# wq loaded first, output sums in two column groups of 288, and the output stored as two plain halves

## The chip, the cores and the metric

The kernel runs on one core of one Trainium2 chip. The core has a matrix engine (PE), a vector engine (DVE), a scalar engine (ACT), GpSimd (POOL) and a sync engine (SP), each with its own instruction queue, and 16 DMA engines that move data between the off-chip memory and the on-chip memory SBUF. PE writes its sums to a second on-chip memory, PSUM. The metric is the device time of one launch in microseconds (us). The kernel before takes 134.05 us, the median of three runs (133.94 to 134.16).

## What is computed

A decode step for two sequences (B = 2, one token each, D = 576): a layer norm, then attention over a sliding block of a cached K and V, plus a dense block with a squared ReLU, plus the input itself.

```python
xn = _layernorm(x)                                   # (2, 1, 576)
# A: 32 query heads of 128, 16 K/V heads, the last W = 2048 of 8192 cached positions
q = (xn @ wq).reshape(B, Sq, Hq, Dh).transpose(0, 2, 1, 3)
k = jnp.repeat(k_cache[:, :, Sk - W:, :], rep, axis=1)
v = jnp.repeat(v_cache[:, :, Sk - W:, :], rep, axis=1)
p = softmax(einsum("bhqd,bhkd->bhqk", q, k) * Dh ** -0.5)
o = einsum("bhqk,bhkd->bhqd", p, v)
a = o.transpose(0, 2, 1, 3).reshape(B, Sq, Hq * Dh) @ wo
# B: F = 4608
h = xn @ w1 + b1
b = square(relu(h)) @ w2 + b2
return x + a + b
```

All inputs and the output are bf16. K and V of the block are 2 x 16.8 MB, wq and wo 4.7 MB each, w1 and w2 5.3 MB each: 53.6 MB are read for one output of 2 x 576.

## The kernel before

**Units.** K and V are worked on in eight units (NU = 8), each one batch entry and four K/V heads: 2048 positions x 4 heads x 128, a tile of 128 partitions x 16 KB (2 MB) for K and one for V. K and V tiles share a pool of six buffers (`kvpool`, line 85), so a load into a buffer waits until what it held has been used. `load_k` and `load_v` (lines 110 to 114) issue them on SP's queue.

**The queue of loads.** All large loads go on SP's queue in the order of the program. It begins (lines 130 to 136) with k0, wq, k1, v0, k2, v1, k3; v2 and k4 follow after units 0 and 1, and so on. A load carries a wait where its buffer is still in use or where the completion semaphore that it takes from a rotating set of eight is still held by an earlier transfer; what stands behind it on SP waits too. wq, w1 and wo use one buffer in turn (`wbig`, one buffer): w1 goes out when the query products are done, wo (line 435) when the products with w1 are done. Then come the two halves of w2: w2a (18 rows of 576), w2b (9 rows) and w2c in three pieces (6, 2 and 1 rows; W2P, line 76).

**Small transfers.** ACT issues x (line 125), four transfers for b1 (lines 417 and 418), one for b2, and the output (lines 455 and 457). Line 455 stores some of w2b to the output first, and line 457 then overwrites it with the result.

**Order on PE.** Every matmul and transpose is kept in program order. The program runs: the transposes of unit 0 (lines 409 and 410), the query block (`q_block`, lines 226 to 255: 36 products with wq, the rows copied, four transposes, eight copies that place the queries into qz), the scores of unit 0, its softmax, then the steps of units 1 to 6. In a step (`step`, line 387) the K tile is transposed in eight groups (line 264, copied out by ACT and DVE in turn at lines 270 and 272), the products with V of the unit two back are put in between (`pv`), and the scores and the softmax of the unit follow. `mlp_h` (line 356) does the products with w1, squares them and transposes them into hT_sb. After step 7, `pv_all` finishes the last two units, and each unit's result is written to ws (line 351).

**The output sums.** `out_acc` (lines 216 to 219) adds one row of wo or w2, a product of 576 columns, to the sums in PSUM. It splits the 576 columns into four quarters of 144 (OQ, line 81) and gives each to another group of 32 columns of the PE array, so that four products run beside each other; quarter i lands on partitions 32i and up. The two batch entries stand 16 rows apart (BS, MB; lines 78 and 79), so the left operands ws, hT_sb and sel_b have 17 columns, of which 15 are zero. The sums of b2 and x start the accumulation (line 422). Lines 445 to 451 do the 32 rows of wo, the 18 rows of w2a and the 18 rows of w2b and w2c. ACT then casts the 113 x 144 sums to bf16 (line 456), and one transfer of eight pieces of 288 bytes writes them out (line 457).

Of the kernel before, what the change touches and what calls it, by code (L numbers as in the profile page):

```python
# [8 lines left out]
F32 = mybir.dt.float32  # L9
BF16 = mybir.dt.bfloat16  # L10
ACT = mybir.ActivationFunctionType
ALU = mybir.AluOpType
AX = mybir.AxisListType
# [3 lines left out]
def kernel(  # L17
# [14 lines left out]
    nc = tc.nc  # L32
    P = 128
    B, Sq, D = A_x.shape
    _, Hkv, Sk, Dh = A_k_cache.shape
# [25 lines left out]
    NG4 = 4  # L61
# [10 lines left out]
    WR = Hq * Dh // P  # L72
    WC = Dh // WR
    FR = L1 // P
    assert HW == 32 * FR and QH * 2 == NC and NC * WC == 32
    W2P = [(9, 15), (15, 17), (17, 18)]
    R9 = 9
    BS = 16
    MB = BS * (B - 1) + 1
    RM = 32 * (NG4 - 1) + MB  # L80
    OQ = D // 4
    BIG = 1e30

    const = ctx.enter_context(tc.tile_pool(name="const", bufs=1))
# [4 lines left out]
    work = ctx.enter_context(tc.tile_pool(name="work", bufs=2))  # L89
    keep = ctx.enter_context(tc.tile_pool(name="keep", bufs=2))  # L90
    psum = ctx.enter_context(tc.tile_pool(name="psum", bufs=1, space=bass.MemoryType.PSUM))

    def matmul(*a, **k):
        tc.keep_in_program_order(nc.tensor.matmul(*a, **k))  # L94
# [5 lines left out]
    out2d = out.rearrange("b s d -> (b s) d")  # L100
# [9 lines left out]
    def load_k(u):  # L110
        issue_kv(k_tiles, A_k_cache, u, "k")
# [4 lines left out]
    def issue_flat(w, name):  # L116
        n = w.shape[0] * w.shape[1] // P
        tl = wbig.tile([P, NH * L1], BF16, tag="wbig", name=name)
        nc.sync.dma_start(out=tl[:, 0:n], in_=w.rearrange("r n -> (r n)").rearrange("(p l) -> p l", p=P))
        return tl  # L120
# [6 lines left out]
    nc.vector.memset(eps_t[:], 1e-5)  # L127
    warm = const.tile([B, 2], F32, name="warm")
    nc.scalar.activation(out=warm[:, 0:1], in_=eps_t[:], func=ACT.Sqrt)
    load_k(0)  # L130
    wq_sb = issue_flat(A_wq, "wq")
    load_k(1)
    load_v(0)
    load_k(2)
# [14 lines left out]
    ident = const.tile([P, P], BF16, name="ident")  # L149
    nc.vector.tensor_scalar(out=ident[:], in0=col_f, scalar1=row_f[:, 0:1], scalar2=None, op0=ALU.is_equal)  # L150
    ident_f = const.tile([P, P], F32, name="ident_f")
    nc.vector.tensor_scalar(out=ident_f[:], in0=col_f[:], scalar1=row_f[:, 0:1], scalar2=None, op0=ALU.is_equal)
    sel_b = const.tile([B + 1, MB], BF16, name="sel_b")
    nc.vector.memset(sel_b[:], 0.0)
    nc.vector.memset(sel_b[:, 0:MB:BS], 1.0)
    nc.vector.tensor_copy(out=sel_b[0:B, 0:MB:BS], in_=ident[0:B, 0:B])

    half_d = D // 2
    stats = const.tile([B, 2, 6], F32, name="stats")
# [50 lines left out]

    w2c_sb = w2pool.tile([P, (FR - R9) * D], BF16, name="w2c")

    out_ps = psum.tile([RM, OQ], F32, tag="out", name="out_ps")
    nc.vector.memset(out_ps[:], 0.0)

    def out_acc(lhsT, rhs, o, start=False, stop=False):
        for i in range(4):
            matmul(out_ps[32 * i:32 * i + MB, :], lhsT=lhsT, rhs=rhs[:, o * D + i * OQ:o * D + (i + 1) * OQ],
                   start=start, stop=stop, skip_group_check=True, tile_position=(0, 32 * i))

    qz = const.tile([P, NQ, B, 2, 3 * QZ], BF16, name="qz")
    nc.gpsimd.memset(qz[:], 0.0)
    q_ps = psum.tile([P, QW], F32, tag="o", name="q_ps")
    nc.vector.memset(q_ps[:], 0.0)

    def q_block():
        for t in range(NH):
            for g in range(NG4):
                o = t * LQ + g * QW
                matmul(q_ps[32 * g:32 * g + 2 * B, :], lhsT=xnT[:, t].rearrange("p x b -> p (x b)"),  # L230
                       rhs=wq_sb[:, o:o + QW], start=(t == 0), stop=(t == NH - 1), skip_group_check=True,
                       tile_position=(0, 32 * g))
        row_t = const.tile([RB, 4 * HW], BF16, tag="row", name="qrow")
        qrow = row_t[:, 0:2 * QW]
        nh = QH // 2
        for k in range(2):
            cp = nc.scalar.copy if k else nc.vector.tensor_copy
            cp(out=qrow[:, k * QW:(k + 1) * QW].rearrange("p (i a d) -> p i a d", a=2, d=Dh),  # L238
               in_=q_ps[0:RB, k * QW // 2:(k + 1) * QW // 2].rearrange("p (i d) -> p i d", d=Dh).unsqueeze(2)
               .to_broadcast([RB, nh, 2, Dh]))  # L240
        qrow_f = qrow.bitcast(F32)
        qT_ps = psum.tile([P, QH * P], F32, tag="sc", bufs=2, name="qT_ps")
        for i in range(QH):
            transpose(out=qT_ps[:, i * P:i * P + RB], in_=qrow_f[:, i * Dh:(i + 1) * Dh],
                      identity=ident_f[0:RB, 0:RB])
        qT_v = qT_ps[:].bitcast(BF16).rearrange("p (i g e x b c) -> p b x g c e i", g=NG4 // 2, e=2, x=32 // B, b=B, c=2)
        hd = Dh // 2
        for j2 in range(2):
            cp = nc.scalar.copy if j2 else nc.vector.tensor_copy
            pp = slice(hd * j2, hd * (j2 + 1))  # L250
            o = QZ + NC * j2
            for b in range(B):
                for half in range(2):
                    cp(out=qz[pp, half * NQ // 2:(half + 1) * NQ // 2, b, :, o:o + NC].rearrange(  # L254
                        "p g c (e i) -> p g c e i", e=2), in_=qT_v[pp, b, half])
# [50 lines left out]
        pT_tiles[u] = pT  # L306
        o1_tiles[u] = o1

    ws = const.tile([P, WR, MB], BF16, name="ws")
    nc.gpsimd.memset(ws[:], 0.0)  # L310
    hT_sb = const.tile([P, 2, FR, MB], BF16, name="hT_sb")
    nc.gpsimd.memset(hT_sb[:], 0.0)

    def pv(u, part, parts):
        n = NJJ // parts
# [10 lines left out]
    def pv_end(u):  # L326
        tq, b = divmod(u, B)
        o_ps = o_tiles.pop(u)
        o1 = o1_tiles.pop(u)
        for k in range(NS):  # L330
            kw = dict(out=o1[:, 0:Dh], in0=o_ps[:, k * Dh:(k + 1) * Dh])
            if k == 0:
                nc.vector.tensor_scalar(scalar1=in_s[:, 0:1], scalar2=None, op0=ALU.mult, **kw)
            else:
                nc.vector.scalar_tensor_tensor(scalar=in_s[:, k:k + 1], in1=o1[:, 0:Dh], op0=ALU.mult, op1=ALU.add,  # L335
                                               **kw)

        def fin():
            op = psum.tile([P, Dh + 1], F32, tag="op", name=f"op_ps_{u}")
            pp = slice(32 * tq, 32 * (tq + 1))  # L340
            matmul(op[pp, :], lhsT=of_h[:], rhs=o1[:], start=True, stop=True, skip_group_check=True,
                   tile_position=(0, 32 * tq))
            linv = work.tile([P, 1], F32, tag="linv", name=f"linv_{u}")
            nc.vector.reciprocal(out=linv[pp, :], in_=op[pp, Dh:Dh + 1])
            om_t = work.tile([P, Dh], F32, tag="om", name=f"om_{u}")
            om = om_t[pp, :].rearrange("p (q r) -> p q r", r=WR)
            nc.vector.scalar_tensor_tensor(out=om, in0=op[pp, 0:Dh].rearrange("p (q r) -> p q r", r=WR),
                                           scalar=linv[pp, 0:1], op0=ALU.mult, op1=ALU.mult,
                                           in1=own_c[pp, :].unsqueeze(2).to_broadcast([32, WC, WR]))
            with nc.allow_low_precision(reason="sums of one term and zeros"):  # L350
                nc.vector.tensor_reduce(out=ws[pp, :, BS * b], in_=om.rearrange("p q r -> p r q"), axis=AX.X,  # L351
                                        op=ALU.add)

        return fin

    def mlp_h(w1_sb):
# [19 lines left out]
        nr = FR // 2  # L376
        for a in range(2):
            hp = psum.tile([P, nr, RB + 4], BF16, tag="sc", bufs=2, name=f"hp_{a}")
            for r in range(nr):
                transpose(out=hp[:, r, 0:RB], in_=hrow[:, a * nr + r:4 * HW:FR], identity=ident[0:RB, 0:RB])  # L380
            for g in range(NG4):
                pp = slice(32 * g, 32 * (g + 1))
                cp = nc.scalar.copy if g % 2 else nc.vector.tensor_copy
                cp(out=hT_sb[pp, :, a * nr:(a + 1) * nr, 0:MB:BS].rearrange("p x r b -> p r x b"),
                   in_=hp[pp, :, 32 * g:32 * g + 2 * B].rearrange("p r (x b) -> p r x b", b=B))

    def step(u):
# [17 lines left out]
    def pv_all(u):  # L405
        pv(u, 0, 1)
        pv_end(u)()

    for g in range(NG):
        transposes(0, g)  # L410
    q_block()
    for t in range(NT):
        scores(0, t)
    softmax(0)
    load_v(2)
    b1_rows = B_b1.rearrange("(x n) -> x n", n=HW)
    for i0, i1 in ((0, 2), (2, 4), (4, 6), (6, 8)):
        nc.scalar.dma_start(out=b1_sb[i0:i1, :], in_=b1_rows[i0:i1, :])
    nc.scalar.dma_start(out=xb_sb[B:B + 1, :], in_=B_b2.rearrange("(o n) -> o n", o=1))
    step(1)  # L420
# [21 lines left out]
    step(NU - 1)  # L442
    pv_all(NU - 2)
    pv_all(NU - 1)
    for r in range(WR):
        out_acc(ws[:, r, :], wo_sb, r)
    for r in range(FR):
        out_acc(hT_sb[:, 0, r, :], w2a_sb, r)
    for r in range(FR):
        w, o = (w2b_sb, r) if r < R9 else (w2c_sb, r - R9)  # L450
        out_acc(hT_sb[:, 1, r, :], w, o, stop=(r == FR - 1))

    fin_sb = work.tile([RM, OQ], BF16, tag="fin", name="fin_sb")
    out_v = out2d.rearrange("b (q n) -> q b n", q=4)
    nc.scalar.dma_start(out=out_v, in_=w2b_sb[0:RM:BS, 0:OQ])
    nc.scalar.copy(out=fin_sb[:], in_=out_ps[:])  # L456
    nc.scalar.dma_start(out=out_v, in_=fin_sb[0:RM:BS, :])


# [28 lines left out]
```

## Time and profile before

| what | value |
|---|---|
| median of three runs | 134.05 us (133.94 to 134.16) |
| span of the profiled execution | 132.06 us (shown as 132.1) |
| mean granted clock of PE | 0.834 |
| busy: PE, DVE, ACT, POOL | 84.6, 63.2, 46.7, 4.9 us |
| read from off-chip memory | 53.62 MB, 406 GB/s over the span |
| share of the large loads' queue | 95.2% of 16 engines' span |
| instruction fetches (queue q8) | 7 packets, 0.11 MB |
| unit 0: transposes, scores done | 8.08 to 14.37 us, 27.20 us |
| wq lands, query products | 19.2 us, 19.23 to 23.27 us |
| products with wo start | 118.36 us |
| cast of the sums, store issued | 129.29, 129.60 us |

The profile is one execution of the program on the chip. Its span runs from the first to the last instruction; a run's device time is about 2 us longer than the span. Times are in us from the start of the span unless marked ns. PE is the matmul stream and PEld the weight loads that run beside it; SP's and ACT's own transfers are listed as SPq and ACTq. A timeline line gives start, length, engine, line, operation, output <- inputs, shapes and count, and in brackets how long the engine was idle before it and what ended that. A line by stretches gives the stretch in us, its length, the busy time of PE, PEld, DVE, ACT and POOL (with the number of instructions), the granted clock of PE as a share of full speed, the busy share of the DMA engines and GB/s. The busy time of PE is made of modelled ends, so overlapping products count once.

### The profile page before, as it was taken

What the parts mean: (1) busy time and instruction counts of PE and PEld (TensorE: products, weight loads), DVE (VectorE), ACT (ScalarE), POOL (GpSimd) and SP (SyncE); (2) the same over time, 40 slices, a digit from 0 to 9 for tenths busy, and PEclk for the clock granted to TensorE, in tenths of its full rate; (3) what the DMA queues carried; (4) which work ended last, traced back from release to release, by engine and by line L of the source; (5) the groups of instructions that cost most, each with busy time, mean ns of one, the idle gap of its engine ahead of it and who ended that gap; (6) DMA issues with size and microseconds to landing.
All of it is one profiled execution on the core that took longest, in us unless ns stands there. A gap on an engine that the chain in (4) does not pass through costs nothing.

```text
span 132.1 us, 2285 instructions
## 1 busy us (share of the span) xinstructions
PE 84.6 (64%) x949; PEld 52.6 (40%) x949; DVE 63.2 (48%) x176; ACT 46.7 (35%) x67; POOL 4.9 (4%) x15
## 2 busy tenths in 40 slices
PE   0089319599589687697599787104819972739471
PEld 0069202286345353363455443002417640229360
DVE  7764400344557677396547687410075667550000
ACT  5725400339566085283256094200106632000000
POOL 5000000010010100100100100100000001000000
PEclk9999955959999999999779999855695999555955
DMA  4999899999999999999999999999999999899960
GB/s 160 397 437 526 369 388 442 422 432 432 429 432 422 442 417 427 437 432 437 432 427 414 437 488 402 445 424 405 427 427 442 468 435 458 376 408 418 418 255 1
DMA packets 3511, 53.76 MB, mean 407 GB/s; under 512 B 419, under 2 KB 558, under 8 KB 814
## 3 DMA queue, kind: packets, MB, share of 16 engines
q1 hardware_dynamic: 3456, 53.61, 95.2%
q8 instruction: 7, 0.11, 0.3%
q10 hardware_dynamic: 46, 0.02, 0.1%
q14 instruction: 2, 0.02, 0.0%
HBM read 53.62 MB, written 0.00 MB: 406 GB/s over the span
## 4 chain that ended last, share of the span: by engine, by line
DMA 78%; PE 15%; ACT 2%; SPq 1%; DVE 1%; issue 1%; ACTq 0%; DVEq 0%
DMA w<-in_B_w_dram 25%; DMA w2c<-in_B_w_dram 24%; DMA k<-in_A_k_cache_dram 16%; DMA wq<-in_A_wq_dram 13%; PE kT_ps L97 5%; PE h_ps L94 3%; PE q_ps L94 3%; PE sc_ps L94 2%; PE out_ps L94 1%; PE o_ps L94 1%; ACT kT L270 1%; DVE qrow L238 1%; SPq L106 0%; ACT qrow L238 0%; DVE qz L254 0%
## 5 line engine op out<-in xcount | busy, mean ns | idle before, releaser
L97 PE MATMUL kT_ps<-ident_f,k 128*128 128x128 f32 x256 | 41.4, 312 | 5.7 <-DMA k<-in_A_k_cache_dram 3.9
L97 PEld LDWEIGHTS kT_ps<-ident_f,k 128*128 128x128 f32 x256 | 32.9, 161 | 18.8 <-issue 9.9
L270 ACT COPY kT<-kT_ps 128x1024 bf16<-128x1024 bf16 x32 | 31.9, 1012 | 17.8 <-PE kT_ps L97 17.8
L272 DVE COPY kT<-kT_ps 128x1024 bf16<-128x1024 bf16 x32 | 21.8, 682 | 6.4 <-PE kT_ps L97 6.1
L94 PE MATMUL sc_ps<-kT,qz 128*32 128x512 bf16 x128 | 9.9, 388 | 6.7 <-DVE kT L272 4.7
L302 ACT ACTIVATE p<-sc_ps,bias 128x512 bf16<-128x512 f32 x8 | 5.5, 688 | 21.4 <-DVE gown L298 18.2
L94 PE MATMUL o_ps<-v,pT 128*32 128x512 bf16 x128 | 11.2, 429 | 0.0
L94 PEld LDWEIGHTS <-xnT 128*4 128x4 bf16 x108 | 3.5, 121 | 16.8 <-issue 15.2
L94 PE MATMUL h_ps<-w,xnT 128*4 128x288 bf16 x72 | 4.3, 429 | 8.0 <-DMA w<-in_B_w_dram 8.0
L305 DVE STREAM_TRANSPOSE pT<-p 128x512 bf16<-128x512 bf16 x8 | 5.7, 710 | 6.2 <-ACT p L302 6.2
L335 DVE SCALAR_TENSOR_TENSOR o<-o_ps,in_s,o 128x128 f32<-128x128 f32 x24 | 8.3, 345 | 0.4
L291 DVE TENSOR_REDUCE m<-sc_ps 128x1 f32<-128x512 f32 x8 | 5.5, 692 | 4.8 <-PE sc_ps L94 4.8
L375 DVE TENSOR_TENSOR hrow<-t 100x1152 bf16<-100x1152 f32 x2 | 2.6, 1355 | 9.6 <-ACT t L373 9.6
L94 PE MATMUL q_ps<-wq,xnT 128*4 128x512 bf16 x36 | 4.0, 627 | 4.9 <-DMA wq<-in_A_wq_dram 4.9
L295 POOL PARTITION_ALL_REDUCE gmax<-m x8 | 2.9, 367 | 104.9 <-DVE m L293 104.9
L94 PE MATMUL op_ps<-o,of_h 128*32 128x129 f32 x16 | 3.7, 316 | 4.6 <-DVE o L335 4.6
L456 ACT CAST fin_sb<-out_ps 113x144 bf16<-113x144 f32 x1 | 0.3, 280 | 17.9 <-PE out_ps L94 17.9
L94 PEld LDWEIGHTS <-qz 128*32 128x32 bf16 x128 | 2.1, 94 | 10.4 <-DVE kT L272 7.2
L97 PE MATMUL pro_ps<-ident,xn_sb 2*128 2x2 bf16 x5 | 0.9, 182 | 6.8 <-DVE xn_sb L171 6.5
L94 PEld LDWEIGHTS <-hT_sb 128*17 128x17 bf16 x144 | 3.4, 108 | 3.6 <-issue 3.5
L94 PE MATMUL out_ps<-wo,ws 128*17 128x144 bf16 x128 | 4.0, 325 | 1.2 <-DVE ws L351 1.2
L238 DVE CAST qrow<-q_ps 100x512 bf16<-100x512 f32 x1 | 0.7, 692 | 8.2 <-PE q_ps L94 8.2
(71 smaller groups left out, 57.4 us busy)
## 6 DMA issues: line engine op xcount, KB each, us to landing
k<-in_A_k_cache_dram SPq DMA_DIRECT2D x8, 2048.0 KB, 21.0
v<-in_A_v_cache_dram SPq DMA_DIRECT2D x8, 2048.0 KB, 21.5
w<-in_B_w_dram SPq DMA_DIRECT2D x1, 5184.0 KB
wq<-in_A_wq_dram SPq DMA_DIRECT2D x1, 4608.0 KB, 17.8
wo<-in_A_wo_dram SPq DMA_DIRECT2D x1, 4608.0 KB
w2a<-in_B_w_dram SPq DMA_DIRECT2D x1, 2592.0 KB, 26.9
w2b<-in_B_w_dram SPq DMA_DIRECT2D x1, 1296.0 KB
w2c<-in_B_w_dram SPq DMA_DIRECT2D x1, 864.0 KB
```

The lines of the kernel that those rows point to most:

```text
L94: tc.keep_in_program_order(nc.tensor.matmul(*a, **k))
L97: tc.keep_in_program_order(nc.tensor.transpose(*a, **k))
L238: cp(out=qrow[:, k * QW:(k + 1) * QW].rearrange("p (i a d) -> p i a d", a=2, d=Dh), in_=q_ps[0:RB, k * QW // 2:(k + 1) * QW // 2].rearrang ...
L270: nc.scalar.copy(out=kT, in_=kT_ps[:])
L272: nc.vector.tensor_copy(out=kT, in_=kT_ps[:])
L291: nc.vector.tensor_reduce(out=m1[:], in_=sc_ps[:], axis=AX.X, op=ALU.max)
L295: nc.gpsimd.partition_all_reduce(gmax[:], m2[:], channels=P, reduce_op=ReduceOp.max)
L302: nc.scalar.activation(out=p_sb[:], in_=sc_ps[:], func=ACT.Exp, bias=bias[:, 0:1], scale=scale, accum_out=o1[:, Dh:Dh + 1])
L305: nc.vector.transpose(out=pT[:].rearrange("p j r -> p (j r)"), in_=p_sb[:])
L335: nc.vector.scalar_tensor_tensor(scalar=in_s[:, k:k + 1], in1=o1[:, 0:Dh], op0=ALU.mult, op1=ALU.add, **kw)
L375: nc.vector.tensor_tensor(out=h4[:, :, k * HB:(k + 1) * HB], in0=t4, in1=t4, op=ALU.mult)
L456: nc.scalar.copy(out=fin_sb[:], in_=out_ps[:])
```

## The change

- wq is loaded ahead of k0 on SP's queue. `q_block` is cut into `q_rows` (the products with wq) and `q_place` (the rest), and both run ahead of the transposes of unit 0.
- The four transfers for b1 become three (rows 0-3, 3-6, 6-8).
- The 16-row distance of the batch entries goes: ws, hT_sb and sel_b have 2 columns and no zeros, and the two memsets of ws and hT_sb on POOL go with them.
- `out_acc` splits a row into two halves of 288 columns on two groups of the array. The even rows of wo and w2a go to out_ps (partitions 0 and 32), the odd rows to a second tile, pre_ps (partitions 64 and 96), which is cleared by DVE.
- After the last row of w2a, ACT copies pre_ps to SBUF (pre_sb, cleared by POOL before), and two fp32 products with columns of the fp32 identity add it to out_ps.
- The rows of w2b and w2c all go to out_ps, on two groups. Between them stand three products of 512 columns into a tile that nothing reads (spin_ps).
- The sums are 34 x 288. The output goes as two transfers of two rows each, the first half on ACT's queue, the second on SP's; the earlier store of w2b into the output covers the first half only.

```diff
+    HD = D // 2
+    RO = 32 + B
+    RP = 96 + B
...
+    wq_sb = issue_flat(A_wq, "wq")
     load_k(0)
-    wq_sb = issue_flat(A_wq, "wq")
     load_k(1)
...
-    out_ps = psum.tile([RM, OQ], F32, tag="out", name="out_ps")
+    out_ps = psum.tile([RO, HD], F32, tag="out", name="out_ps")
     nc.vector.memset(out_ps[:], 0.0)
-    def out_acc(lhsT, rhs, o, start=False, stop=False):
-        for i in range(4):
-            matmul(out_ps[32 * i:32 * i + MB, :], lhsT=lhsT, rhs=rhs[:, o * D + i * OQ:o * D + (i + 1) * OQ],
-                   start=start, stop=stop, skip_group_check=True, tile_position=(0, 32 * i))
+    def out_acc(lhsT, rhs, o, start=False, stop=False, acc=out_ps, base=0):
+        for i in range(2):
+            p = base + 32 * i
+            matmul(acc[p:p + B, :], lhsT=lhsT, rhs=rhs[:, o * D + i * HD:o * D + (i + 1) * HD], start=start,
+                   stop=stop, skip_group_check=True, tile_position=(0, p))
...
-    ws = const.tile([P, WR, MB], BF16, name="ws")
-    nc.gpsimd.memset(ws[:], 0.0)
-    hT_sb = const.tile([P, 2, FR, MB], BF16, name="hT_sb")
-    nc.gpsimd.memset(hT_sb[:], 0.0)
+    ws = const.tile([P, WR, B], BF16, name="ws")
+    hT_sb = const.tile([P, 2, FR, B], BF16, name="hT_sb")
...
+    q_rows()
+    q_place()
     for g in range(NG):
         transposes(0, g)
-    q_block()
...
-    for i0, i1 in ((0, 2), (2, 4), (4, 6), (6, 8)):
+    for i0, i1 in ((0, 3), (3, 6), (6, 8)):
         nc.scalar.dma_start(out=b1_sb[i0:i1, :], in_=b1_rows[i0:i1, :])
...
+    pre_ps = psum.tile([RP, HD], F32, tag="sc", bufs=2, name="pre_ps")
+    nc.vector.memset(pre_ps[:], 0.0)
+    pre_sb = work.tile([P, HD], F32, tag="t1", name="pre_sb")
+    nc.gpsimd.memset(pre_sb[:], 0.0)
+    spin_ps = psum.tile([P, 512], F32, tag="sc", bufs=2, name="spin_ps")
+
+    def out_alt(lhsT, rhs, r, start=False, stop=False):
+        if r % 2:
+            out_acc(lhsT, rhs, r, start=start, stop=stop, acc=pre_ps, base=64)
+        else:
+            out_acc(lhsT, rhs, r)
+
     for r in range(WR):
-        out_acc(ws[:, r, :], wo_sb, r)
+        out_alt(ws[:, r, :], wo_sb, r, start=(r == 1))
     for r in range(FR):
-        out_acc(hT_sb[:, 0, r, :], w2a_sb, r)
+        out_alt(hT_sb[:, 0, r, :], w2a_sb, r, stop=(r == FR - 1))
+    nc.scalar.copy(out=pre_sb[64:RP, :], in_=pre_ps[64:RP, :])
+    for i in range(2):
+        p = 64 + 32 * i
+        matmul(out_ps[32 * i:32 * i + B, :], lhsT=ident_f[:, p:p + B], rhs=pre_sb[:], start=False, stop=False,
+               skip_group_check=True, tile_position=(0, 32 * i))
     for r in range(FR):
         w, o = (w2b_sb, r) if r < R9 else (w2c_sb, r - R9)
         out_acc(hT_sb[:, 1, r, :], w, o, stop=(r == FR - 1))
+        if r == R9 - 1:
+            for _ in range(3):
+                matmul(spin_ps[0:B, :], lhsT=ws[:, 0, :], rhs=wo_sb[:, 0:512], start=True, stop=True,
+                       skip_group_check=True)
-    fin_sb = work.tile([RM, OQ], BF16, tag="fin", name="fin_sb")
-    out_v = out2d.rearrange("b (q n) -> q b n", q=4)
-    nc.scalar.dma_start(out=out_v, in_=w2b_sb[0:RM:BS, 0:OQ])
+    fin_sb = work.tile([RO, HD], BF16, tag="fin", name="fin_sb")
+    nc.scalar.dma_start(out=out2d[:, 0:HD], in_=w2b_sb[0:B, 0:HD])
     nc.scalar.copy(out=fin_sb[:], in_=out_ps[:])
-    nc.scalar.dma_start(out=out_v, in_=fin_sb[0:RM:BS, :])
+    nc.scalar.dma_start(out=out2d[:, 0:HD], in_=fin_sb[0:B, :])
+    nc.sync.dma_start(out=out2d[:, HD:D], in_=fin_sb[32:RO, :])
```

More of the change, by code (lines that the diff above doesn't have):

```diff
@@ L77 @@
     R9 = 9
[L78 to L81, printed above, removed]
+    HD = D // 2
+    RO = 32 + B
+    RP = 96 + B
     BIG = 1e30
@@ L152 @@
     nc.vector.tensor_scalar(out=ident_f[:], in0=col_f[:], scalar1=row_f[:, 0:1], scalar2=None, op0=ALU.is_equal)
[L153 to L156, printed above, removed]
+    sel_b = const.tile([B + 1, B], BF16, name="sel_b")
+    nc.vector.memset(sel_b[:], 1.0)
+    nc.vector.tensor_copy(out=sel_b[0:B, :], in_=ident[0:B, 0:B])
     half_d = D // 2
@@ L224, with q_rows @@
     nc.vector.memset(q_ps[:], 0.0)
-    def q_block():
+    def q_rows():
         for t in range(NH):
@@ L232, in q_block, with q_place @@
                        tile_position=(0, 32 * g))
+    def q_place():
         row_t = const.tile([RB, 4 * HW], BF16, tag="row", name="qrow")
@@ L350, in fin @@
             with nc.allow_low_precision(reason="sums of one term and zeros"):
-                nc.vector.tensor_reduce(out=ws[pp, :, BS * b], in_=om.rearrange("p q r -> p r q"), axis=AX.X,
+                nc.vector.tensor_reduce(out=ws[pp, :, b], in_=om.rearrange("p q r -> p r q"), axis=AX.X,
                                         op=ALU.add)
@@ L383, in mlp_h @@
                 cp = nc.scalar.copy if g % 2 else nc.vector.tensor_copy
-                cp(out=hT_sb[pp, :, a * nr:(a + 1) * nr, 0:MB:BS].rearrange("p x r b -> p r x b"),
+                cp(out=hT_sb[pp, :, a * nr:(a + 1) * nr, :].rearrange("p x r b -> p r x b"),
                    in_=hp[pp, :, 32 * g:32 * g + 2 * B].rearrange("p r (x b) -> p r x b", b=B))
```

## The prediction

> **What bounds the kernel now.** I read the busy shares by slice first, then the chain that ended last.
>
> ```profile
> span 132.1 us, 2285 instructions
> PEclk9999955959999999999779999855695999555955
> DMA  4999899999999999999999999999999999899960
> GB/s 160 397 437 526 369 388 442 422 432 432 429 432 422 442 417 427 437 432 437 432 427 414 437 488 402 445 424 405 427 427 442 468 435 458 376 408 418 418 255 1
> DMA 78%; PE 15%; ACT 2%; SPq 1%; DVE 1%; issue 1%; ACTq 0%; DVEq 0%
> ```
>
> The transfer engines are full from the second slice to the last but two: 53.6 MB at about 430 GB/s. PE, DVE and ACT only have to keep up. What they do counts in two places: where a late consumer would leave the queue without work, and behind the last landing. The timeline and the tile view show that tail:
>
> ```profile
> 118.36 4.02 PE L94 MATMUL out_ps<-wo,ws 128*17 128x144 bf16 x128 [1.16 <-DVE ws L351]
> 122.73 1.05 PE L94 MATMUL out_ps<-w2a,hT_sb 128*17 128x144 bf16 x54 [0.35 <-DMA w2a<-in_B_w_dram]
> 125.29 0.48 PE L94 MATMUL out_ps<-w2a,hT_sb 128*17 128x144 bf16 x18 [1.51 <-issue]
> 125.82 1.26 PE L94 MATMUL out_ps<-w2b,hT_sb 128*17 128x144 bf16 x36
> 127.90 1.34 PE L94 MATMUL out_ps<-w2c,hT_sb 128*17 128x144 bf16 x36 [0.82 <-DMA w2c<-in_B_w_dram]
> L94 PE MATMUL out_ps<-w2c,hT_sb x36: 278/327/328, 127.9 to 129.0; 128*17 128x144 bf16 x36
> 125.80 0.65 ACTq L455 DMA_DIRECT2D out_dram<-w2b  x1
> 129.29 0.28 ACT L456 CAST fin_sb<-out_ps 113x144 bf16<-113x144 f32 x1 [17.85 <-PE out_ps L94]
> 129.60 0.54 ACTq L457 DMA_DIRECT2D out_dram<-fin_sb  x1
> ```
>
> PE has spare time here: it waits for w2a (0.35), for its own instructions (1.51, "issue") and for w2c (0.82). The w2b tile lands by 125.80, when the dummy store that reads it (L455) goes out. The 36 w2c products pace at 30 ns, so 1.08 us of work took 1.34: they waited inside for the second and third piece. The last four start at 129.0, so I put the last landing at 128.9 (an estimate from that start).
>
> Last, the same tail cut at the borders where the granted clock changes, and one earlier stretch:
>
> ```profile
> 115.48:118.90 3.42, 1.15 (x22) 0.76 (x26) 1.80 (x6) 0.00 (x0) 0.00 (x0) 0.50 0.94 406
> 118.90:122.31 3.41, 3.41 (x116) 3.27 (x109) 0.00 (x0) 0.00 (x0) 0.00 (x0) 0.50 0.98 420
> 122.31:125.72 3.41, 1.54 (x76) 1.15 (x72) 0.00 (x0) 0.00 (x0) 0.00 (x0) 1.00 0.98 409
> 125.72:129.14 3.42, 2.55 (x74) 2.08 (x71) 0.00 (x0) 0.00 (x0) 0.00 (x0) 0.50 0.55 215
> 129.14:132.10 2.96, 0.11 (x4) 0.00 (x0) 0.00 (x0) 0.28 (x1) 0.00 (x0) 0.50 0.00 1
> 50.63:54.04 3.41, 2.00 (x18) 0.89 (x16) 2.19 (x6) 1.01 (x1) 0.00 (x0) 1.00 0.99 423
> ```
>
> The first number after the stretch is its length, the next PE's busy time; 0.50 or 1.00 ahead of the last two is the granted clock. The clock steps every 3.41 us. At half clock a full stretch (3.41) lifts the next one to 1.00; 2.55, three quarters, did not. At full clock 1.54 (45%) dropped the next to 0.50, while after 2.00 (59%) it stayed at 1.00.
>
> **The change, part by part.** Times are in the profiled execution (span 132.06); the median of the runs is 134.05, so 1.99 us lie outside the span, taken as unchanged.
>
> *wq ahead of k0.* Same bytes on SP's queue. k0 and wq together landed at 19.2; at 430 GB/s k0's 2.1 MB are 4.9 us, so wq alone lands near 14.3. Query products (4.0, as now) end at 18.3; the placing took 25.98-23.27 = 2.7, to 21.0. Unit 0's transposes follow the last query transpose, near 20.1, and with their copies took 15.1-8.1 = 7.0: to 27.1. The scores (1.2, plus 0.4 for the mask product) end near 28.6 against 27.2: 1.4 us late. Queued behind on SP, v2 waits for the transposes of unit 0 (26.5 for 19.27) and k4 for those of unit 1 (about 35 for 33.63). At 33.63 19.4 MB have been issued and some 13.2 landed (31.5 us at 0.42 MB/us), so 6.2 MB or 14 us of transfers still cover a delay of 1.4. PE wins it back: it waits 0.32 for k at 44.77 and 1.22 at 54.63. Cost 0; if the cover were gone, +1.4. The b1 transfers, three for four, each saves some 0.3 us of issue on ACT at 4.4 us, where nothing waits: 0.
>
> *Smaller ws, hT_sb, sel_b.* Two POOL memsets (0.55 and 0.61) and one on DVE go, all in the first 2.5 us under the first load: 0. Two memsets are added: pre_ps on DVE (about 0.3, from 485 ns for 128x512) in unit 7 between accumulations, where DVE idles 0.78 before L344, and pre_sb on POOL, which idles: 0.
>
> *Two column groups.* The wo and w2a rows alternate between groups 0/1 and 2/3, four groups as before: half as many products of double width. From h_ps, 72 products of 288 columns in four groups in 4.30 us at half clock: 60 ns each, 240 alone. So wo is 64 x 60 = 3.84 (was 4.02), w2a 36 x 30 = 1.1 at full clock (the 72 ran at some 20 ns). The 1.51 "issue" is a wait for the instruction stream; 262 fewer loads and products in the tail may remove it (gain 0 to 1.51, all in PE's slack). The last half stays on two groups: 120 ns a product at half clock, 61 at full, against 2 x 30 and 2 x 16 before. w2b is 18 x 61 = 1.1 or 18 x 120 = 2.2; w2c the same.
>
> *Join.* ACT copies 34x288 (0.40: L373 does 100x288 in 404 to 411 ns), then two fp32 products. op_ps, 129 fp32 columns, took 0.41 at full clock, some 0.24 above a product's 0.17 tail (223 ns less 144 columns at 2.4 a ns, twice the 288 in 240 above); 288 columns make 0.53 + 0.17 = 0.7 if the two groups overlap, 1.2 if not. From w2a's end at 124.0: copy to 124.5, join to 125.2 or 125.7. That is before w2b lands at 125.80: 0. At half clock it ends at 126 to 127.
>
> *Three spin products.* 512 columns in one group: 427 ns at half clock (36 of q_ps in 4.0 on four groups), 213 at full. At full clock 125.8 + 1.1 + 0.64 = 127.5, under the landing at 127.9: 0. Then w2c: twelve products 0.73 to 128.6, when piece two is due, four to 128.9, and the last pair on the last landing as now. Its latency: 286 ns (288 columns, full) for 290 (144, half): 0.
>
> *Cast and store.* 34x288 for 113x144: from 280 ns (144) to 586 (512) is 0.83 ns a column, +0.12. The store's way from issue to landing: now 129.60 to between 131.2 and 131.4 (SP waits 2.3 us for it from the last w2c piece; POOL's closing starts at 131.4). A plain two-row transfer on ACT, xb_sb, was issued at 0.73 and SP went on behind it at 2.19: 1.46, 0.15 to 0.35 less. For the half on SP I have only issue times, 0.33 (L441) to 0.63 (the first k), against 0.54: -0.21 to +0.09, plus a hand-over of 0.05. Both halves must land. Ends -0.35 and +0.14; nearest is xb_sb, halved for the second half: -0.1.
>
> On the second queue the Trainium skill ("DMA: Bandwidth & Descriptors", Issuing engines are not separate DMA queues) speaks against a gain: two issuers save only issue time. By it the store's term would be 0 and the sum +0.12; no row here shows two stores at once.
>
> Sum: 0.12 - 0.1 = +0.02, so **134.1**. Its own range: -0.35+0.12 = -0.23 to 0.14+0.12+0.15 (last pair at half clock, 444 ns as in h_ps) = +0.41, and 0.11 of spread between runs: 133.7 to 134.6. Within 0.2% (0.27 us), about what a measurement can tell from none, I call no change.
>
> **The rivals.**
>
> *The clock is at half under w2b and w2c (slower).* That is the condition of the sum: PE's own time decides once the w2c products can't end by 129. If the clock falls only for w2c: 127.9 + 18 x 0.12 + 0.17 = 130.23 for 129.24, +1.0: 135.1. From w2b on: 125.8 + 2.16 + 1.28 of spin + 2.16 + 0.17 = 131.57, +2.35: 136.4. For it: in the profile the clock does stand at 0.50 from 125.72, harmless only because four groups hid it; the borders need not fall at the same place in each run, and a wo block of 3.9 us just fills one stretch of 3.41. If the lift needs over nine tenths, a border in mid-block misses it. Against: with the shorter idle times, w2a, join, w2b, spins and w2c make 1.25+0.7 busy in 122.3-125.7 (57%, near the 59% that held) and some 3.0 of 3.41 in the next. 0.35.
>
> On this the Trainium skill ("TensorE: Matmul & The Clock Gate", Part 1) drops the clock only after an idle window of about 3.4 us. By it the clock would hold from 122.3 on and the sum stand; the row at 45%, with no pause over 1.51, speaks otherwise, and the row decides.
>
> *The stream ends earlier (faster).* Instructions come over the same engines: seven packets, 0.3% of 16 engines' span (0.003 x 16 x 132.1 / 7 = 0.9 us of one engine each). With fewer of them the engine that ends last may end 0.9 earlier: 133.2; if they hit others, 0. 0.09.
>
> *The front's delay isn't won back.* +1.4 where the queue runs dry: 135.4; 14 us of issued work speak against it. 0.03.
>
> **How the numbers follow.** The sum's case has 0.53: 0.16 faster, 0.27 within, 0.10 slower (it runs from -0.34 to +0.52, the zone of no change in its middle). Clock 0.35, slower; early stream 0.09, faster; front 0.03, 0.02 of it slower and 0.01 within. Faster 0.25, same 0.28, slower 0.47. The range takes the first case, its faster edge and the clock's prices: 133.6 to 136.4.
>
> **What would show it.** w2c products start at 127.9 and the cast at 129.3, granted clock 1.00 from 125.8: the sum. A cast after 130 with 0.50: the clock. A w2c landing well before 127.9: the stream. DMA below 9 in slices 8 to 20: the front. Wrong altogether: a 288-column product on two groups slower than 61 ns, a join beyond 125.8, or an issue wait in the tail.

## The result and the profile after

| | kernel before | changed kernel |
|---|---|---|
| median (runs) | 134.05 us (5; 133.94 to 134.19) | 134.73 us (5; 134.61 to 134.88) |
| ratio to before, with 95% interval | | 1.0051 (1.0039 to 1.0063) |
| span of the profiled execution | 132.06 us | 132.74 us |
| last landing of the large loads, from the packet records | 128.56 us | 129.34 us |
| from there to the end of the span | 3.50 us | 3.40 us |
| mean granted clock of PE | 0.834 | 0.897 |

The changed kernel is slower by 0.68 us, 0.5%. The forecast of 134.1 was too low by 0.6 us; the range held the time. The two rows on the last landing (the end of the last packet of the large loads) already say where to look: behind it the change gains 0.10 us, and it comes 0.78 us later itself.

The page of the changed kernel, cut to the lines that were shown of before (span, shares by slice, the chain by engine):

```profile
span 132.7 us, 2025 instructions
PEclk9999999999999869999999999955595999655899
DMA  6898999999999999999999999998999999899970
GB/s 178 389 490 368 416 439 430 439 415 439 407 425 434 425 439 410 425 425 434 434 407 430 410 490 425 430 434 378 434 420 444 480 389 489 367 419 406 407 273 1
DMA 75%; PE 14%; ACT 5%; SPq 1%; issue 1%; DVE 1%; ACTq 0%; DVEq 0%
```

There are 260 instructions fewer and PE's clock is higher, but the transfer engines are as full as before and the chain that ended last still consists mostly of transfers (75%, before 78%). Nothing on this page names the loss. The tail (the products with w2 and what follows them), from the timeline of the changed kernel (start, length, engine, line, work, idle time before it):

```profile
123.48 0.40 PE L93 MATMUL out_ps<-w2a,hT_sb 128*2 128x288 bf16 x2 [0.48 <-DMA w2a<-in_B_w_dram]
...
125.09 0.39 ACT L461 COPY pre_sb<-pre_ps 34x288 f32<-34x288 f32 x1 [12.71 <-PE pre_ps L93]
125.54 0.65 PE L93 MATMUL out_ps<-pre_sb,ident_f 128*2 128x288 f32 x4 [0.56 <-ACT pre_sb L461]
126.61 0.26 ACTq L475 DMA_DIRECT2D out_dram<-w2b  x1
126.63 1.27 PE L93 MATMUL out_ps<-w2b,hT_sb 128*2 128x288 bf16 x18 [0.43 <-DMA w2b<-in_B_w_dram]
127.73 0.81 PE L93 MATMUL spin_ps<-wo,ws 128*2 128x512 bf16 x3
128.75 1.40 PE L93 MATMUL out_ps<-w2c,hT_sb 128*2 128x288 bf16 x18 [0.21 <-DMA w2c<-in_B_w_dram]
130.19 0.39 ACT L476 CAST fin_sb<-out_ps 34x288 bf16<-34x288 f32 x1 [4.70 <-PE out_ps L93]
130.61 0.33 SPq L478 DMA_DIRECT2D out_dram<-fin_sb  x1
130.61 0.25 ACTq L477 DMA_DIRECT2D out_dram<-fin_sb  x1
```

Each step waits for its load: w2a (0.48), w2b (0.43), w2c (0.21). The join ends at 126.19, before w2b's products; the spins end at 128.54, before w2c lands. The whole row is the one forecast, shifted: w2a 0.75, w2b 0.8 and w2c 0.85 later than before. The clock in this tail, by the stretches at whose borders it may change (columns as before: length, busy times of PE, PEld, DVE, ACT, POOL, granted clock, DMA share, GB/s):

```profile
120.58:123.99 3.41, 2.93 (x56) 1.55 (x48) 0.00 (x0) 0.00 (x0) 0.00 (x0) 0.50 0.96 404
123.99:127.40 3.41, 2.42 (x50) 1.26 (x44) 0.00 (x0) 0.39 (x1) 0.00 (x0) 1.00 0.99 400
127.40:130.81 3.41, 2.54 (x30) 1.24 (x25) 0.00 (x0) 0.39 (x1) 0.00 (x0) 1.00 0.30 113
```

The clock is 1.00 under the join, w2b, the spins and w2c, so the prediction's rival of a half clock did not happen.

Now the stream. These are products that wait for a load, in the kernel before:

```profile
54.63 1.06 PE L97 MATMUL kT_ps<-ident_f,k 128*128 128x128 f32 x8 [1.22 <-DMA k<-in_A_k_cache_dram]
74.12 1.06 PE L97 MATMUL kT_ps<-ident_f,k 128*128 128x128 f32 x8 [0.28 <-DMA k<-in_A_k_cache_dram]
91.09 4.27 PE L94 MATMUL h_ps<-w,xnT 128*4 128x288 bf16 x72 [7.96 <-DMA w<-in_B_w_dram]
```

and in the changed kernel:

```profile
54.94 1.06 PE L96 MATMUL kT_ps<-ident_f,k 128*128 128x128 f32 x8 [0.59 <-DMA k<-in_A_k_cache_dram]
74.56 1.06 PE L96 MATMUL kT_ps<-ident_f,k 128*128 128x128 f32 x8 [1.84 <-DMA k<-in_A_k_cache_dram]
91.67 4.49 PE L93 MATMUL h_ps<-w,xnT 128*4 128x288 bf16 x72 [8.78 <-DMA w<-in_B_w_dram]
```

Each starts at a landing, and the same landing is late by 0.31, then 0.44, then 0.58 us, then 0.75 for w2a. That is no pause at one place: from each of these points to the next the transfers are slower by 0.5 to 0.8%. The packet records (one for each piece that a transfer engine moves) say it directly. A K or V tile is 128 packets of 16 KB, eight for each of the 16 engines. From the 16th us on a packet took 611 ns in the kernel before; in the changed kernel 611 ns up to about 25 us and 615.7 ns after 40 us (means without the few packets that an instruction fetch held up). The packets of w1 rose from 1533.0 to 1537.8, those of wo from 1364.0 to 1368.6: 4.6 to 4.8 ns on each of these three sizes. The smaller packets of w2 rose by amounts from 0.5 ns (1152 bytes) to 8.2 ns (10368 bytes, 389.2 to 397.4). Some 165 packets per engine follow the 25th us; what they took longer, added up size by size, is 0.72 us of the 0.78.

Nor is it the engines that disturb the transfers. This stretch of the changed kernel has no work on any of them:

```profile
85.95:88.95 3.00, 0.00 (x0) 0.00 (x0) 0.00 (x0) 0.00 (x0) 0.00 (x0) 0.58 0.96 415
```

and yet w1's packets took 1539 ns in the mean between 86 and 89 us, against 1533 before.

What differs for a packet? Its bytes do not, and behind the first loads their order does not either. Its destination does. ws, hT_sb and sel_b lost 2080 bytes per partition, and everything allocated behind the constants moved down by that much: K and V buffers from byte 31232 of a partition (122 x 256) to 29152 (113 x 256 + 224), all with the same remainder since a buffer is 16 KB. The destinations of wq, w1, wo, w2b and w2c have that remainder too; w2a's went from 128 to 96. The unused tile `pad_0` (576 bytes, line 122 before, 121 after) lies ahead of the constants, so its size sets these addresses and nothing else.

### The profile page after: what moved, and what is told of

The parts are those of the page before. It is cut to its first block, busy times and chain, and to the rows that moved or that the text cites. A ratio compares the mean times of both kernels' runs of the same rounds, so it can differ in the third digit from the quotient of the medians.

```text
span 132.7 us, 2025 instructions
## 1 busy us (share of the span) xinstructions
PE 82.7 (62%) x818; PEld 45.7 (34%) x818; DVE 63.1 (48%) x176; ACT 46.7 (35%) x68; POOL 4.2 (3%) x14
## 4 chain that ended last, share of the span: by engine, by line
DMA 75%; PE 14%; ACT 5%; SPq 1%; issue 1%; DVE 1%; ACTq 0%; DVEq 0%
DMA w<-in_B_w_dram 25%; DMA w2c<-in_B_w_dram 23%; DMA k<-in_A_k_cache_dram 16%; DMA wq<-in_A_wq_dram 10%; PE kT_ps L96 4%; PE h_ps L93 3%; ACT kT L271 3%; PE q_ps L93 3%; PE sc_ps L93 2%; PE out_ps L93 1%; ACT L303 1%; PE o_ps L93 1%; DVE qrow L239 1%; ACT qrow L239 0%; SPq L105 0%
## 5 line engine op out<-in xcount | busy, mean ns | idle before, releaser
L96 PE MATMUL kT_ps<-ident_f,k 128*128 128x128 f32 x256 | 38.0, 290 | 7.6 <-DMA k<-in_A_k_cache_dram 5.6
L96 PEld LDWEIGHTS kT_ps<-ident_f,k 128*128 128x128 f32 x256 | 28.6, 146 | 22.1 <-issue 12.3
L93 PE MATMUL o_ps<-v,pT 128*32 128x512 bf16 x128 | 11.7, 451 | 0.0
L239 ACT CAST qrow<-q_ps 100x512 bf16<-100x512 f32 x1 | 0.6, 586 | 13.3 <-DVE qrow L239 13.3
L332 DVE TENSOR_SCALAR o<-o_ps,in_s 128x128 f32<-128x128 f32 x8 | 2.8, 346 | 5.1 <-PE o_ps L93 5.1
```

The lines of the kernel that those rows point to most:

```text
L96: tc.keep_in_program_order(nc.tensor.transpose(*a, **k))
```

## The experiments

Theory A: the packets became slower by their destination, that is, by the byte of a partition at which a load starts. Theory B: by the front, the new order at the start (wq first, K unit 2 held behind it), which might shift the 16 engines against each other. Medians are of 5 to 12 runs; the kernel before, run beside them, took 134.00, 134.01 and 134.02 us in the three sets.

**1. The changed kernel, tiles back on the old remainder.**

```diff
-    const.tile([P, 144], F32, name="pad_0")
+    const.tile([P, 536], F32, name="pad_0")
```

> The changed kernel with the unused pad of the constants' pool widened from 576 to 2144 bytes a partition, so that every K, V and weight tile starts 1568 bytes higher, on the same offset within 512 bytes as in the kernel before (0 for K and V; the changed kernel has 480). The instructions and their order are those of the change. Theory A (the stream's packets became slower since the smaller constants moved the destinations off 512-byte boundaries): the 16 KB packets take 611 ns all through, the last load lands about 0.8 us earlier, near 128.5 us of the span, and the time is about 133.95 us. Theory B (the new front, wq first and K unit 2 held back behind it, changed the phase of the 16 engines): packets of 617 ns after 26 us as in the change, 134.7 us.

133.75 us, ratio 0.9983 (0.9974 to 0.9992); last landing 128.55, packets of 611.0 ns. Waits for the same landings, and the end, in its timeline:

```profile
54.47 1.06 PE L96 MATMUL kT_ps<-ident_f,k 128*128 128x128 f32 x8 [0.24 <-DMA k<-in_A_k_cache_dram]
74.08 1.94 PE L96 MATMUL kT_ps<-ident_f,k 128*128 128x128 f32 x8 [1.91 <-DMA k<-in_A_k_cache_dram]
91.15 4.49 PE L93 MATMUL h_ps<-w,xnT 128*4 128x288 bf16 x72 [6.15 <-DMA w<-in_B_w_dram]
...
127.87 1.35 PE L93 MATMUL out_ps<-w2c,hT_sb 128*2 128x288 bf16 x18 [0.15 <-DMA w2c<-in_B_w_dram]
129.26 0.39 ACT L476 CAST fin_sb<-out_ps 34x288 bf16<-34x288 f32 x1 [4.07 <-PE out_ps L93]
```

The landings are those of the kernel before again (54.63, 74.12, 91.09, 127.90). An unused tile's size alone brings 0.98 us (0.91 by the two ratios to the kernel before, each run beside its own set) and puts the change on the other side of the kernel before.

**2. The kernel before, everything moved by 32 bytes.**

```diff
-    const.tile([P, 144], F32, name="pad_0")
+    const.tile([P, 136], F32, name="pad_0")
```

> The kernel before with the unused pad made 32 bytes smaller, so that K and V tiles start at offset 480 within 512 bytes, as the changed kernel has them; nothing else differs. Theory A (destination offsets): packets lengthen from 611 to about 617 ns, and the time rises to about 134.8 us. Theory B (order of the front): 134.05 us, within 0.15.

134.88 us, ratio 1.0068 (1.0055 to 1.0082); packets of 615.6 ns. The loss of the change without any of its work: theory A.

**3 and 4. The front taken out of the change, and put alone into the kernel before.** Number 3 has the order of the kernel before:

```diff
-    wq_sb = issue_flat(A_wq, "wq")
     load_k(0)
+    wq_sb = issue_flat(A_wq, "wq")
...
-    q_rows()
-    q_place()
     for g in range(NG):
         transposes(0, g)
+    q_rows()
+    q_place()
...
-    for i0, i1 in ((0, 3), (3, 6), (6, 8)):
+    for i0, i1 in ((0, 2), (2, 4), (4, 6), (6, 8)):
```

> The changed kernel with its front put back (K unit 0 ahead of wq, the q block behind the transposes of unit 0, the bias in four transfers), its smaller constants, its two column groups and its two-halves store kept. Theory A (destination offsets): still about 134.7 us, packets of 617 ns. Theory B (order of the front): 133.95 us, packets of 611 ns.

Number 4 is the reverse edit on the kernel before, whose `q_block` moves whole.

> The kernel before with only the front of the change (wq ahead of K unit 0, the q block ahead of the transposes of unit 0, the bias in three transfers); its constants, and so every tile's place, stay. Theory A (destination offsets): 134.05 us within 0.15, packets of 611 ns. Theory B (order of the front): about 134.8 us, packets of 617 ns after 26 us.

Number 3: 134.78 us, ratio 1.0059 (1.0046 to 1.0072), packets of 615.7 ns. Number 4: 133.95 us, ratio 0.9996 (0.9987 to 1.0005), packets of 611.0 ns. The slow packets go with the addresses and not with the front. Theory B falls.

**5. Only the destinations of the loads moved.** The kernel before with one unused 32-byte tile between the constants and the K/V buffers, and one behind the weights' buffers, so that the engines' own tiles move by 64 bytes and the constants not at all.

```diff
+    shift0 = ctx.enter_context(tc.tile_pool(name="shift0", bufs=1))
+    shift0.tile([P, 8], F32, name="shift_0")
     kvpool = ctx.enter_context(tc.tile_pool(name="kvpool", bufs=6))
...
+    shift1 = ctx.enter_context(tc.tile_pool(name="shift1", bufs=1))
+    shift1.tile([P, 8], F32, name="shift_1")
     ktpool = ctx.enter_context(tc.tile_pool(name="ktpool", bufs=2))
```

> The kernel before with two unused pads of 32 bytes, one ahead of the K and V buffers and one behind the weights' buffers: the destinations of the loads move by 32 bytes, the constants not at all, and the tiles that only the engines use by 64. Theory A (the destinations of the loads): about 134.88 us, as when everything moved by 32 bytes. Rival (what slows is an engine's read or write of its own tiles off a 64-byte boundary, or their clash with the loads): 134.0 us.

134.89 us, ratio 1.0064 (1.0052 to 1.0077), packets of 615.6 ns. Its waits for w1 and w2c:

```profile
91.64 4.07 PE L98 MATMUL h_ps<-w,xnT 128*4 128x288 bf16 x72 [7.79 <-DMA w<-in_B_w_dram]
...
128.72 1.39 PE L98 MATMUL out_ps<-w2c,hT_sb 128*17 128x144 bf16 x36 [0.87 <-DMA w2c<-in_B_w_dram]
```

These are the changed kernel's landings (91.67, 128.75) in the old kernel. The constants stayed, so it is the destinations of the loads. One rival isn't excluded by this run alone: the engines' own tiles moved by 64 bytes, and the engines read the loaded tiles at their new places. Against it stands the stretch from 85.95 us above, in which no engine worked and the packets were slow all the same.

**6 to 8. Which boundary.** The changed kernel with `pad_0` of 168, 184 and 216 floats.

> The changed kernel with its unused pad 96 bytes wider, so that K and V tiles start at offset 64 within 512 bytes (the changed kernel: 480; the widened one run before: 0). Theory A1 (a multiple of 64 bytes is enough for a destination): packets of 611 ns and about 133.75 us, as with offset 0. Theory A2 (only a multiple of 512, or of more than 64, will do): about 134.7 us.

> The changed kernel with its unused pad 160 bytes wider: K and V tiles start at offset 128 within 512 bytes. If a multiple of 128 bytes is enough (w2a's destination lies at offset 128 in the kernel before, and its packets of 20736 bytes took 771 ns there as in the widened kernel): 133.75 us, packets of 611 ns. If the step is at 512 bytes, or the cost falls off slowly with the offset's size: between 134.0 and 134.4 us.

> The changed kernel with its unused pad 288 bytes wider: K and V tiles start at offset 256 within 512 bytes. If a multiple of 128 or of 256 bytes is enough: 133.75 us. If only a multiple of 512 is: 134.0 to 134.4 us.

Together with the others, sorted by where in 256 bytes a K or V buffer starts:

| K/V start, remainder by 256 | kernel | 16 KB packets, ns | last landing, us | time, us | ratio to before (95%) |
|---|---|---|---|---|---|
| 0 | widened pad (1) | 611.0 | 128.55 | 133.75 | 0.9983 (0.9974 to 0.9992) |
| 0 (256 by 512) | pad 216 | 611.0 | 128.61 | 133.78 | 0.9975 (0.9966 to 0.9984) |
| 32 | loads moved (5) | 615.6 | 129.35 | 134.89 | 1.0064 (1.0052 to 1.0077) |
| 64 | pad 168 | 614.8 | 129.20 | 134.42 | 1.0031 (1.0019 to 1.0043) |
| 128 | pad 184 | 614.5 | 129.14 | 134.41 | 1.0022 (1.0009 to 1.0034) |
| 224 | the change | 615.7 | 129.34 | 134.73 | 1.0051 (1.0039 to 1.0063) |

The case "64 is enough" did not come true, and neither did "128 is enough". A multiple of 256 bytes costs nothing; 64 and 128 cost 3.5 to 3.8 ns a packet of 16 KB and about 0.65 us; 224, on the same instructions, 0.98 us. (Row 32 has the old instructions; number 2 is 224 on the old instructions, with 615.6 ns and 134.88 us.) It is the remainder and not the place: the fast starts 29440, 30720 and 31232 lie among slow ones, from 29152 (the change) to 31264 (number 5).

**9. Without the spins**, on the widened pad: the loop of three products is left out.

```diff
-        if r == R9 - 1:
-            for _ in range(3):
-                matmul(spin_ps[0:B, :], lhsT=ws[:, 0, :], rhs=wo_sb[:, 0:512], start=True, stop=True,
-                       skip_group_check=True)
```

> The changed kernel with the wide pad (133.75 us) without the three spin products between w2b and w2c. If the spins keep the clock: TensorE falls to half speed within 4 us of w2b's products, w2c's 18 products take about 2.0 in place of 1.4 us, and the time rises by 0.3 to 0.6 us, to 134.05 to 134.35. If the work of w2a, the join and w2b holds the clock by itself, or the last landing decides anyway: 133.75 within 0.15.

133.74 us (133.64 to 133.83 over 11 runs), ratio 0.9979 (0.9971 to 0.9988), against 133.75 with them. In its profile the clock was 1.00 from 121.65 to 131.89 without any spin. The spins change nothing here that these runs can tell.

**10. Without the second sum**, on the widened pad: all rows go straight to out_ps, no copy, no join.

```diff
-        if r % 2:
-            out_acc(lhsT, rhs, r, start=start, stop=stop, acc=pre_ps, base=64)
-        else:
-            out_acc(lhsT, rhs, r)
+        out_acc(lhsT, rhs, r)
```

> The changed kernel with the wide pad (133.75 us), with all rows of wo and w2a summed in the two column groups of the output, no second sum, no copy and no joining products. If the odd rows in groups of their own are needed: wo's 26 rows take 0.24 us each at half clock, some 6.2 us from about 120, w2a's 18 rows end about 128 and not 125.5, w2b's products follow late by 1 us or more, and the time is 134.0 to 135. If two groups suffice, since w2b and w2c are waited for anyway: 133.75 within 0.15.

134.38 us, ratio 1.0030 (1.0017 to 1.0043), 0.63 above its partner. The profiled execution is the longest of its eight (134.78 us; they run from 134.15), so its delays are larger than those of the median. From its timeline:

```profile
118.64 6.71 PE L93 MATMUL out_ps<-wo,ws 128*2 128x288 bf16 x64 [1.06 <-DVE ws L350]
125.19 2.37 PE L93 MATMUL out_ps<-w2a,hT_sb 128*2 128x288 bf16 x36
...
127.39 1.27 PE L93 MATMUL out_ps<-w2b,hT_sb 128*2 128x288 bf16 x18
...
130.46 0.39 ACT L464 CAST fin_sb<-out_ps 34x288 bf16<-34x288 f32 x1 [18.22 <-PE out_ps L93]
```

Behind the products with wo no line of PE has a wait in brackets: on two groups the rows of wo take 6.71 us (the prediction had 3.84 for four groups), those of w2a and w2b queue up behind them, and the cast is at 130.46 in place of 129.26. Alternating the rows over four groups is what lets two wide groups do in the rest of the tail.

**11. The tail without the front**, on the widened pad.

> The changed kernel with the wide pad and the front of the kernel before (K unit 0 ahead of wq, the q block behind the transposes, the bias in four transfers): what is left of the change is the two column groups, the join, the spins and the store, with every load on the offset of the kernel before. If the tail alone brings the 0.25 us of the widened kernel: 133.75 to 133.85 us. If the front brings it (the new front alone gave 133.95 against 134.00): 133.95 to 134.05.

133.94 us, ratio 0.9991 (0.9983 to 0.9999). On good addresses there are then four kernels: neither part 134.00 to 134.02, front alone 133.95, tail alone 133.94, both 133.75. Number 11 falls between the two cases of its expectation. The intervals are about 0.12 us wide to each side, so the front alone can't be told from nothing, the tail alone barely, and that both together bring 0.25 and not the 0.13 of their sum isn't clear of the noise either.

## Why the prediction missed, and why its range held

**The step that failed** is the line "Smaller ws, hT_sb, sel_b: ... 0", together with "Same bytes on SP's queue ... Cost 0". The first counted the memsets that go and not the 2080 bytes that go, which set the address of every load behind them; the second took equal bytes for equal time. In their place the runs show +0.98 us from the destination alone (the changed kernel against number 1), 0.7% of the time of a kernel that waits for its loads nearly throughout; the rest of the change brings -0.25 us (number 1 against the kernel before). The Trainium skill ("DMA: Bandwidth & Descriptors", How a descriptor splits into AXI transactions) describes such a boundary, for reads: a transaction has at most 256 bytes and must start on a multiple of 256, so that a descriptor which doesn't start there takes bytes that it doesn't use. The forecast drew on that page for the store and not for the loads. The runs agree on the boundary, for destinations in SBUF; on the size they don't follow the page's count of 32-byte beats, by which remainder 32 would be the cheapest and 224 the dearest, while 32 and 224 cost 4.6 and 4.7 ns on a packet of 16 KB, and 64 and 128 3.5 to 3.8.

**That the range held is luck.** The sum's own range ended at 134.6. The stated one reached to 136.4, and slower had the largest chance, for a half clock under w2b and w2c, which none of the eight profiles with the new tail and the join shows. The time lies in the range, and on its likeliest side, for a cause that stands in none of its cases.

**The sum behind the last landing was right in kind.** Forecast +0.02 (-0.23 to +0.41). From the last landing to the end, the four kernels profiled with the old tail took 3.50 to 3.63 us, mean 3.56, the eight with the new tail and the join 3.24 to 3.49, mean 3.35: -0.21, at the lower end. By terms, in the changed kernel: the cast +0.11 (0.28 to 0.39; forecast +0.12). The store, from issue to the end of the span, went from 132.06 - 129.60 = 2.46 to 132.74 - 130.61 = 2.13, so -0.33, near this term's lower bound of -0.35; I had taken -0.1. Whether this comes from two pieces in place of eight or from the second queue wasn't separated. Two readings of the kernel before were off, without weight for the result. The last landing, put at 128.9 by the start of the last four products, was at 128.56 by the packets: those products start at 128.95, 0.39 behind their last packet. And 131.57 us for the half clock from w2b on is 2.33 above 129.24, not 2.35.

**The join was hidden**, as forecast: 0.39 + 0.65 us, done 0.44 before w2b. The 1.51 us of "issue" in the tail went, which the forecast had left open, and bought nothing, as it lay in slack. w2b's products took 61 ns each at full clock, as forecast.

**The front.** Forecast: unit 0 done 1.4 us later, won back. Its scores ended at 26.76, 0.44 earlier than before (27.20): the query products ended at 18.5 as forecast (18.3), but the transposes and copies of unit 0 took 6.0 us (20.11 to 26.08) and not the 7.0 taken from the kernel before, and the scores ended 0.7 after the last copy, where I had put 1.6 behind it. The cost of 0 was right.

**The rivals.** Half clock (0.35): not in the changed kernel, nor in numbers 1 and 9; in the changed kernel a stretch with 2.93 of 3.41 us busy lifted the clock and one with 2.42 held it. An earlier end by fewer instruction fetches (0.09): the fetches fell from seven to six packets, and at equal addresses the last landing stayed (128.56 before, 128.55 in number 1). The front not won back (0.03): no, as just said.

## What to carry to other kernels

Where transfers bound the kernel, the destination of a load is part of its cost: an edit that resizes any tile moves all that is allocated behind it, so list the addresses before and after and keep the large loads on multiples of 256 bytes. A loss that grows evenly along the stream points to the packets, one that appears at one place to a wait. Measure an edit at equal addresses before judging it: here a change worth -0.25 us (133.75 against 134.00) measured +0.68.

## What the runs showed of the hardware that was not expected

- Off a 256-byte start the large packets pay per packet, not per byte: 4.7, 4.6 and 4.8 ns on packets of 16384, 36864 and 41472 bytes in the changed kernel. Two sizes don't fit. w2b's packets (10368 bytes) rose by 8.2 ns at remainder 224, but by less than 1 ns at 32 and 64 and not at all at 128. w2a's packets (20736 bytes) started at remainder 128 in the kernel before and in number 1, and took 771 ns there, as at remainder 0 (pad 184, 771.4), but 773.8 at 96.
- The slower packets set in late: in the changed kernel they took 611 ns to about 25 us, in number 2 to about 33 us, though the destinations were off from the first. What starts it is open; no run was made for it. So a start off 256 bytes is needed for the slow packets, but it isn't the whole cause.
- The best versions found, on 256-byte starts, with or without the spins, took 133.74 to 133.78 us, below both kernels.
